# Windowed attention and an MLP-mixer: another order of operations and loads, and the last tail rows in two stores

## The chip, the cores and the metric

The kernel runs on one core of one Trainium2 chip. The metric is the device time of one execution in microseconds; the median of three runs stands for the kernel.

## The reference

Sliding-window attention with a linear bias, then a mixer block, for 8 batches of 576 rows, 8 heads of 64 (512 columns):

```python
scores = scale * np.matmul(q, k.transpose(0, 1, 3, 2))     # per batch and head, 576 x 576
mask = (rel >= 0) & (rel < 128)                             # rel = row - column
attn = softmax(np.where(mask, scores + bias[None], -1e9))
x = matmul(attn, v)                                         # back to (batch, 576, 512)
h = np.maximum(xt @ w_tok1, 0.0) @ w_tok2                   # token mix, 576 -> 256 -> 576
u = x + h.transpose(0, 2, 1)
h2 = np.maximum(u @ w_ch1, 0.0) @ w_ch2                     # channel mix, 512 -> 1536 -> 512
out = u + h2
```

## The kernel before

Work runs in blocks of 128 rows. A batch has 576 rows, four blocks and 64 rows over; the spare rows of two batches are joined into one tail block (`TAIL`), so two batches make a pair with nine blocks. All matmuls are in bf16.

For each batch there is a **side** part and a **main** part. The side part takes q and k of each block, transposes them (on TensorE in the opening, L653; later by SP's transposing transfers, L642), computes the scores of a block against itself and the block before it (L693, a 64-row form of the matmul, two heads at once), the exponentials on ScalarE (L716), the mask and bias as one product on DVE (L726), attention times v with a column of ones that gives the row sums (L760), and the normalisation (L773, L776; some of them on ScalarE, L782). Then comes the token mix: L805 and L815 (first layer), a ReLU (L823), L848 (second layer; L844 for the tail block) and the residual sum into the tile `ub` (L866). The tile is then transposed into `uT`, for batches 0 and 1 on TensorE (L883), from batch 2 on by SP (L874).

The main part is the channel mix. The first layer is L1045 (L1030 for the first pieces of batch 0, L967 for the last batch, L1088 for the tail), with its ReLU on L1051. The second layer uses seven half-size products in place of eight (L1234), with sums of the operands made on DVE (L1070) and the results collected in L1202; L1263 is the last product of the last batch, in two halves. The tail block's second layer is L1133, and L1140 adds its residual. Results leave by transfers at L1214, L1150 (tail rows) and L1270 (the last two blocks, one on SP's queue and one on ScalarE's).

Who comes first is not written by hand. A small planner (class `Plan`) holds every operation with its engine, a cost, a rank and its dependences, and plays them through in time: each engine takes the operation that can start first, ties going by rank. The rank is moved by a random offset per group of 30 operations, from the table `SEEDS`. The planner has costs for transfers: `LATE` and `RATES` for the loads that GpSimd (POOL) issues, `TURN` for SP's transposes (duration and lateness, for the uT and the qkT kind), `CASTS` for the first loads. The order that comes out is emitted as it is, one queue for each engine, and each engine then keeps to it. Where the planner expects TensorE to be idle in the first 60 us, it emits filler matmuls on zeros (`spin`, L1319).

POOL issues the loads in the order of the string `LOADS` (L378): `k1` is block 1 of k, `W1` and `W2` the token weights, `A0` to `A3` quarters of the first channel weight `WC1`, `B0` to `B3` of the second, `WC2`; then those of pairs 1 to 3 in a fixed order. At most eight of POOL's transfers are in flight. Each waits for its buffer: there are five for q and k and five for v.

SP's queue holds the transposes and most output stores, in the planner's order: an instruction whose data is not there holds up all behind it. The stores of the tail block go out as two transfers, because its 128 rows belong to two batches. In the last batch the tail block is the last in its list, so it comes in two column halves, with two stores for each.

Of the kernel before, what the change touches and what calls it, by code (L numbers as in the profile page):

```python
# [64 lines left out]
def offset(o):  # L65
    seed = SEEDS.get(o.group, 0)
    z, full = (seed << 20) + o.part * 1000 + o.at, (1 << 64) - 1
    z = (z + 0x9E3779B97F4A7C15) & full
    z = ((z ^ (z >> 30)) * 0xBF58476D1CE4E5B9) & full
    z = ((z ^ (z >> 27)) * 0x94D049BB133111EB) & full  # L70
    return ((z ^ (z >> 31)) >> 11) * 2.0**-52 - 1.0 if seed else 0.0


class Plan:
# [54 lines left out]
    def run(self):  # L129
# [43 lines left out]
        def advance(to):  # L173
            nonlocal clock, flying
            while True:
# [13 lines left out]
                if both:  # L189
                    rate = RATES[0 if not lines[1][0][1].bus else 2 if lines[1][0][1].bus < 1500 else 1]  # L190
                    if getattr(lines[0][0][1], "packets", 0) == 520:
# [18 lines left out]
        def send(o, at, line, work, late):  # L210
            nonlocal flying
            coming.append([at, line, work, o, late])
            flying += 1

        while todo:
# [70 lines left out]
            elif e == "SP":  # L286
                o.t0 = t
                if o.bus:
# [3 lines left out]
                    turns.append(o)  # L292
                    send(o, t + 300, 1, TURN[o.bus > 1500][0], TURN[o.bus > 1500][1])
                else:
                    free[e] = t + 590
                    send(o, t + 300, 1, STORE * o.cost / 550, 1010.0)
            else:
                o.t0 = t
                free[e] = t + o.cost
                send(o, t + o.cost, 0, STORE if o.packets < 0 else o.packets * PACKET, 1010.0 if o.packets < 0 else LATE[t > FETCH])  # L300
                lanes.append(o)
# [8 lines left out]
    def emit(self, spin):  # L310
# [11 lines left out]
        for _, _, go in sorted(work, key=lambda w: w[:2]):  # L322
# [20 lines left out]
RANKH = 0  # L343
RELU = 350
SUMS_AT = 60e3
SEEDS = {0: 846071, 4: 412855, 5: 343328, 6: 901394, 7: 671959, 8: 764867, 10: 416701, 11: 351752, 12: 70309, 20: 619675, 21: 120696, 22: 577973, 23: 405716, 30: 213057, 31: 165847, 32: 71954, 40: 404590, 41: 482568, 50: 286568, 51: 611926, 60: 579527, 61: 819459, 62: 379002, 70: 640395, 71: 934419, 72: 439456, 80: 109511, 81: 910233, 82: 748762, 90: 519950, 91: 197367, 101: 150347, 102: 405724, 110: 7956, 111: 36992, 112: 363882, 120: 129293, 122: 874736, 130: 359970, 131: 803027, 140: 23914, 141: 388902, 142: 496852, 150: 220523, 151: 220010, 152: 75231, 153: 900190}
GROUP = 30
SHIFT = 1500.0
UNIT_LATE = False
# [14 lines left out]
MORE = 150.0  # L364
START = 5200.0
RAW = 3
CASTS = [5000.0, 5680.0, 7560.0, 8040.0]
PACKET = 0.813
LATE = (2400.0, 3500.0)
FETCH = 9000.0  # L370
STORE = 774.0
TURN = [(792.0, 1267.0), (1380.0, 2400.0)]
RATES = [(0.37, 0.23), (0.52, 0.35), (0.47, 0.18)]
HALF = 0.9
EARLY = 1


LOADS = ("k1 q1 k2 q2 v0 k8 q8 v1 v2 v8 v3 W1 q7 q4 k4 W2 q6 "  # L378
         "k6 A0 k7 q5 A3 k5 v7 v4 A1 v6 v5 A2 B0 T0 P1 B2 B1 B3")


@with_exitstack
def kernel(
# [16 lines left out]
    P = nc.NUM_PARTITIONS  # L400
    B, H, S, D = q.shape
# [4 lines left out]
    NC = S // P  # L406
    R = S - NC * P
    NB = 2 * NC + 1
    TAIL = 2 * NC
# [24 lines left out]
    def bank(choice=ONE):  # L434
        return plan.buf("ps", choice)
# [27 lines left out]
    W1 = const.tile([P, NC, DTOK], BF16, name="W1")  # L463
    W1p = const.tile([P, 2, DTOK], BF16, name="W1p")
    W2 = const.tile([P, NJ, NC * P], BF16, name="W2")
# [75 lines left out]
    for i_, raw in enumerate(raws):  # L541
        buf, i = block(0, (0, RAW)[i_ // 2])["qk"], i_ % 2

        def cast(eng=dve_.tensor_copy, raw=raw, buf=buf, i=i):
            eng(out=buf()[:, i, :, :], in_=raw.rearrange("p (h d) -> p h d", h=H))

        plan.op("DVE", (520, 660)[i], cast, -100 + i_, makes=buf, after=CASTS[i_],
                **({"other": ("ACT", 600, lambda cast=cast: cast(act_.copy))} if i_ > 1 else {}))
# [4 lines left out]
    plan.items = []  # L553
    for item in LOADS.split():
        what, n = item[:-1], int(item[-1])
# [461 lines left out]
    def main(b, rank):  # L1017
        pr, half = b // 2, b % 2
# [5 lines left out]
        if b == 0:  # L1024
            first = [bank() for _ in range(PIECES)]
            for blk in blocks:
                for t, ct in enumerate(first):
                    def go(t=t, ct=ct, blk=blk):
                        for cb in range(NCB):
                            pe_.matmul(ct()[:, blk * P : (blk + 1) * P], lhsT=WC1[:, cb, t * P : (t + 1) * P],  # L1030
                                       rhs=uT()[:, cb, blk * P : (blk + 1) * P],
                                       start=cb == 0, stop=cb == NCB - 1)
# [89 lines left out]
        for blk in blocks:  # L1122
            cuts = [slice(0, DM)]
            if b == B - 1 and blk == blocks[-1]:
                cuts = [slice(0, DM // 2), slice(DM // 2, DM)]
            for cols in cuts:
                o2 = bank()
                n = cols.stop - cols.start
                for g in range(NHT // 3):
                    def go(blk=blk, g=g, o2=o2, cols=cols):  # L1130
                        for t in range(3 * g, 3 * g + 3):
                            l = r2t()[:, t, :] if blk == TAIL else r2()[:, t, (blk % NC) * P : (blk % NC + 1) * P]
                            pe_.matmul(o2()[:, cols], lhsT=l, rhs=WC2[:, t, cols], start=t == 0, stop=t == NHT - 1)  # L1133

                    rk = rank(648)
                    rd = [(r2t, g * 3 // 4), (r2t, (g * 3 + 2) // 4)] if blk == TAIL else [(r2, t) for t in range(3 * g, 3 * g + 3)]
                    plan.op("PE", 649 * n / DM, go, rk, reads=rd, needs=lc2[3 * g : 3 * g + 3],
                            **({"makes": o2} if g == 0 else {"adds": o2}))
                ob = plan.buf("ob")
                plan.op("DVE", 160 + 530 * n / DM, lambda blk=blk, o2=o2, ob=ob, cols=cols: dve_.tensor_tensor(  # L1140
                    out=ob()[:, cols], in0=o2()[:, cols], in1=ub()[:, blk, cols], op=ALU.add), rk, makes=ob, uses=[o2],
                    reads=[(ub, blk)])

                late = b >= FROM_P and blk not in blocks[-2:] or FROM_P <= b < B - 1
                q_ = nc.gpsimd if late else nc.sync

                def store(blk=blk, ob=ob, cols=cols, q_=q_):
                    if blk == TAIL:
                        for i in range(2):
                            q_.dma_start(out=out[2 * pr + i, NC * P : S, cols], in_=ob()[i * R : (i + 1) * R, cols])  # L1150
                    else:
                        q_.dma_start(out=out[b, (blk % NC) * P : (blk % NC + 1) * P, cols], in_=ob()[:, cols])

                if late:
                    plan.dma(store, P, -1, uses=ob)
                else:
                    plan.op("SP", 550, store, rk, uses=[ob])
# [197 lines left out]
```

## Time and profile before

| | |
|---|---|
| median of three runs | 278.48 us (277.51 to 278.57) |
| the profiled execution | 277.36 us |
| its span, first to last instruction | 275.6 us |
| instructions | 6968 |
| granted TensorE clock | 1.000 |
| read from and written to HBM | 35.85 MB, 9.44 MB |

The span is what the profile sees; the execution's time has 1.8 us around it. In the profile, PE is TensorE's matmuls, PEld its weight loads, POOL is GpSimd, and SPq is SP's queue. A row of a group gives the source line, engine, operation, tiles written and read, shape and count. A row of a timeline gives the start, the length, and in brackets the idle time of the engine before it. In a row of a line's operations, three times with slashes are the least, the middle and the greatest duration in ns. "DMA to landing" is the time from issue to the last byte's notice. A row of windows gives a stretch, its length, then busy time and count of PE, PEld, DVE, ACT and POOL, the granted clock, the DMA share and GB/s.

### The profile page before, as it was taken

Reading aid. Unit: us, or ns where it says so; the run is one execution under the profiler, and the core shown is the slowest. Engines: PE = TensorE matmul, PEld = TensorE weight load, DVE = VectorE, ACT = ScalarE, POOL = GpSimd, SP = SyncE. Lnnn points to the kernel's source line nnn. Section 1 sums busy time; section 2 is a strip of 40 time slices with the busy share of each in tenths; the row PEclk is TensorE's granted clock in tenths of the full one; section 3 lists DMA queues with packets and bytes.
Section 4 is the critical chain, followed back from the end, with each engine's and each line's share of the span. In section 5 each row is a group of like instructions: output and inputs, shape, how many; then the busy total and the mean of one; then the engine's idle time right before and its main releaser. Section 6 shows DMA issues by size and latency. Waiting matters only on the chain.

```text
span 275.6 us, 6968 instructions
## 1 busy us (share of the span) xinstructions
PE 268.4 (97%) x2790; PEld 180.8 (66%) x2824; DVE 210.3 (76%) x496; ACT 139.1 (50%) x239; POOL 114.0 (41%) x144
## 2 busy tenths in 40 slices
PE   8999999999999999999999999999999999999994
PEld 4665655676676556585658655576676655599983
DVE  7596799987898379956979468763998459967983
ACT  5475893426940388109950187116960089106560
POOL 8898747940454039700891009600462410021000
PEclk9999999999999999999999999999999999999999
DMA  8999999999899899979999859999599760043014
GB/s 156 154 165 178 179 200 183 155 129 210 127 107 130 176 233 142 152 120 193 189 149 148 199 146 95 135 158 242 68 99 126 195 132 0 2 113 137 1 49 145
DMA packets 167553, 38.71 MB, mean 140 GB/s; under 512 B 155808, under 2 KB 166688, under 8 KB 167520
## 3 DMA queue, kind: packets, MB, share of 16 engines
q0 software_dynamic: 114032, 19.77, 91.8%
q1 hardware_dynamic: 51264, 17.83, 33.4%
q10 hardware_dynamic: 2224, 0.66, 1.2%
q8 instruction: 22, 0.36, 0.5%
q14 instruction: 11, 0.09, 0.1%
HBM read 35.85 MB, written 9.44 MB: 164 GB/s over the span
## 4 chain that ended last, share of the span: by engine, by line
PE 81%; DMA 6%; DVE 5%; POOL 4%; issue 2%; SPq 1%; POOLq 0%
PE ps L1234 25%; PE ps L1045 24%; PE ps L760 6%; PE ps L693 5%; DMA qk<-in_k_dram 5%; PE ps L805 4%; PE ps L848 4%; PE ps L1088 4%; PE ps L967 3%; PE ps L1133 3%; DVE pe L726 2%; POOL qk L530 2%; POOL v L530 1%; DMA uT<-ub 1%; PE ps L815 1%
## 5 line engine op out<-in xcount | busy, mean ns | idle before, releaser
L1045 PE MATMUL ps<-uT,WC 128*128 128x512 bf16 x306 | 77.9, 379 | 1.3 <-DMA uT<-ub 0.2
L716 ACT ACTIVATE pe<-ps 128x1024 bf16<-128x1024 f32 (+1 forms) x76 | 63.4, 890 | 19.1 <-PE ps L693 18.8
L530 POOL DMA_DIRECT2D v<-in_v_dram x40 | 34.1, 858 | 91.8 <-PE ps L760 88.6
L1051 ACT ACTIVATE r<-ps 128x512 bf16<-128x512 f32 x77 | 45.0, 604 | 51.4 <-PE ps L1045 49.3
L1045 PEld LDWEIGHTS <-WC 128*128 128x128 bf16 x328 | 29.1, 98 | 29.3 <-issue 0.9
L726 DVE TENSOR_TENSOR pe<-pe,mask 128x1024 bf16<-128x1024 bf16 (+1 forms) x64 | 38.7, 609 | 12.0 <-ACT pe L716 11.5
L1234 PEld LDWEIGHTS <-r 128*128 128x128 bf16 x372 | 36.1, 98 | 7.3
L530 POOL DMA_DIRECT2D qk<-in_k_dram x38 | 33.0, 876 | 4.6 <-DMA WC<-in_moe_w_ch_dram 2.4
L530 POOL DMA_DIRECT2D qk<-in_q_dram x38 | 32.7, 866 | 1.7 <-PE ps L1234 0.7
L1234 PEld LDWEIGHTS <-s 128*128 128x128 bf16 x288 | 27.4, 98 | 6.0 <-issue 2.0
L776 DVE TENSOR_TENSOR xb<-ps,rt 128x256 bf16<-128x256 f32 (+1 forms) x72 | 28.9, 417 | 0.8
L760 PEld LDWEIGHTS <-pe 128*128 128x128 bf16 (+1 forms) x560 | 22.6, 98 | 9.1 <-DVE pe L726 1.3
L760 PE MATMUL ps<-v,pe 128*128 128x65 bf16 (+1 forms) x560 | 26.9, 194 | 0.3
L1234 PE MATMUL ps<-WC,r 128*128 128x256 bf16 x192 | 25.4, 273 | 0.0
L1234 PE MATMUL ps<-WT,s 128*128 128x256 bf16 x192 | 24.8, 273 | 0.0
L866 DVE TENSOR_TENSOR ub<-ps,xb 128x512 bf16<-128x512 f32 x34 | 21.3, 683 | 2.5 <-PE ps L848 2.5
L1234 PE MATMUL ps<-WT,r 128*128 128x256 bf16 x180 | 22.3, 273 | 0.0
L693 PEld LDWEIGHTS <-qkT 64*128 64x128 bf16 x560 | 14.8, 94 | 10.7 <-issue 8.2
L1202 DVE TENSOR_TENSOR raw<-ps,ub 128x512 f32<-128x512 f32 x22 | 15.0, 686 | 8.1 <-PE ps L1234 8.1
L693 PE MATMUL ps<-qkT 64*128 64x128 bf16 (+1 forms) x304 | 19.5, 216 | 0.0
L1093 ACT ACTIVATE r2t<-ps 128x512 bf16<-128x512 f32 x12 | 7.2, 600 | 22.9 <-PE ps L1088 22.7
L773 DVE RECIPROCAL rt<-ps 128x4 f32<-128x4 f32 (+1 forms) x76 | 12.6, 176 | 7.3 <-PE ps L760 6.9
(101 smaller groups left out, 348.1 us busy)
## 6 DMA issues: line engine op xcount, KB each, us to landing
out_dram<-raw SPq DMA_DIRECT2D x18, 256.0 KB, 2.8
v<-in_v_dram POOLq DMA_DIRECT2D x32, 128.0 KB, 5.1
qk<-in_k_dram POOLq DMA_DIRECT2D x30, 128.0 KB, 5.5
qk<-in_q_dram POOLq DMA_DIRECT2D x30, 128.0 KB, 5.1
WC<-in_moe_w_ch_dram POOLq DMA_DIRECT2D x8, 384.0 KB, 9.4
out_dram<-ob SPq DMA_DIRECT2D x5, 256.0 KB, 2.6
out_dram<-ob POOLq DMA_DIRECT2D x4, 256.0 KB, 2.7
out_dram<-raw POOLq DMA_DIRECT2D x4, 256.0 KB, 2.9
```

Source lines behind the costliest of these rows:

```text
L530: nc.gpsimd.dma_start(out=to()[p0 : p0 + n, :, :], in_=rows(src, b, s0, n))
L693: pe_.matmul(wide(e)[:, i, kind, a:z], lhsT=ts[kb]()[e * D : (e + 1) * D, NHP + i, :], rhs=ts[blk]()[e * D : (e + 1) * D, i, a:z], start=n ...
L716: act_.activation(out=pb()[:, e, :, lo:, c0:c1_], in_=wide(e)[:, :, lo:, c0:c1_], func=ACT.Exp, scale=scale)
L726: dve_.tensor_tensor(out=o, in0=o, in1=heads(mk, es), op=ALU.mult)
L760: pe_.matmul(view()[a:z, at, i, :], lhsT=pb()[:, e, i, kind, a:z], rhs=vb()[:, h, 0 : D + 1], start=m == 0, stop=m == len(mms) - 1, skip_g ...
L773: dve_.reciprocal(out=rt()[r0:r1_, 0:n, :, :], in_=view()[r0:r1_, :, :, D : D + 1])
L776: dve_.tensor_tensor(out=x4(), in0=view()[r0:r1_, :, :, 0:D], in1=rt()[r0:r1_, 0:n, :, :].broadcast_to([r1_ - r0, n, 4, D]), op=ALU.mult)
L866: plan.op("DVE", 690, lambda blk=blk, ht=ht, hs=hs: dve_.tensor_tensor(out=ub()[:, blk, :], in0=ht()[:, hs], in1=xb()[:, blk, :], op=ALU.a ...
L1045: pe_.matmul(ct()[:, :], lhsT=WC1[:, cb, t * P : (t + 1) * P], rhs=uT()[:, cb, :], start=cb == 0, stop=cb == NCB - 1)
L1051: plan.op("ACT", 600, lambda t=t, ct=ct: act_.activation(out=r2()[:, t, :], in_=ct()[:, :], func=ACT.Relu), rk, part=(r2, t), uses=[ct], o ...
L1202: dve_.tensor_tensor(out=v, in0=both(bk), in1=src, op=ALU.add)
L1234: pe_.matmul(of(bk, c), lhsT=l(t, c), rhs=w(t), start=first, stop=g == 1 and t == HK - 1, skip_group_check=True)
```

## The change

Three kinds of edit: the table of seeds, which moves ranks and so the order of the operations; some of the planner's costs and the order of the first loads; and the tail store of the last batch, which becomes one transfer for both batches of the pair.

```diff
-SEEDS = {0: 846071, 4: 412855, 5: 343328, 6: 901394, ...}
+SEEDS = {0: 210116, 4: 311062, 5: 744428, 6: 487106, ...}
...
-CASTS = [5000.0, 5680.0, 7560.0, 8040.0]
+CASTS = [4950.0, 5600.0, 7500.0, 8000.0]
 PACKET = 0.813
-LATE = (2400.0, 3500.0)
+LATE = (2400.0, 3300.0)
...
-TURN = [(792.0, 1267.0), (1380.0, 2400.0)]
-RATES = [(0.37, 0.23), (0.52, 0.35), (0.47, 0.18)]
+TURN = [(843.0, 2200.0), (1455.0, 2000.0)]
+RATES = [(0.2, 0.45), (0.47, 0.31), (0.5, 0.13)]
...
-LOADS = ("k1 q1 k2 q2 v0 k8 q8 v1 v2 v8 v3 W1 q7 q4 k4 W2 q6 "
-         "k6 A0 k7 q5 A3 k5 v7 v4 A1 v6 v5 A2 B0 T0 P1 B2 B1 B3")
+LOADS = ("k1 q1 q2 k2 k8 v8 v0 q8 v1 v3 v2 W1 q4 k4 W2 k7 q6 "
+         "q7 A0 k5 k6 v4 A2 v7 q5 A3 v6 P1 T0 v5 A1 B0 B3 B1 B2")
...
                 def store(blk=blk, ob=ob, cols=cols, q_=q_):
-                    if blk == TAIL:
+                    if blk == TAIL and b == B - 1:
+                        q_.dma_start(out=out[2 * pr : 2 * pr + 2, NC * P : S, cols], in_=ob()[:, cols])
+                    elif blk == TAIL:
                         for i in range(2):
                             q_.dma_start(out=out[2 * pr + i, NC * P : S, cols], in_=ob()[i * R : (i + 1) * R, cols])
```

The whole table of seeds is new; what that does can only be seen in the order that comes out. The two added lines move every line behind them by two: L1214 becomes L1216, L1234 becomes L1236, L1319 becomes L1321, and the tail store of the last batch is L1149.

More of the change, by code (lines that the diff above doesn't have):

```diff
@@ L345 @@
 SUMS_AT = 60e3
-SEEDS = {0: 846071, 4: 412855, 5: 343328, 6: 901394, 7: 671959, 8: 764867, 10: 416701, 11: 351752, 12: 70309, 20: 619675, 21: 120696, 22: 577973, 23: 405716, 30: 213057, 31: 165847, 32: 71954, 40: 404590, 41: 482568, 50: 286568, 51: 611926, 60: 579527, 61: 819459, 62: 379002, 70: 640395, 71: 934419, 72: 439456, 80: 109511, 81: 910233, 82: 748762, 90: 519950, 91: 197367, 101: 150347, 102: 405724, 110: 7956, 111: 36992, 112: 363882, 120: 129293, 122: 874736, 130: 359970, 131: 803027, 140: 23914, 141: 388902, 142: 496852, 150: 220523, 151: 220010, 152: 75231, 153: 900190}
+SEEDS = {0: 210116, 4: 311062, 5: 744428, 6: 487106, 7: 50177, 10: 146866, 11: 515882, 12: 973009, 20: 155072, 21: 744920, 22: 317240, 23: 698122, 30: 985153, 31: 625367, 32: 450301, 40: 930871, 41: 214279, 42: 112853, 50: 891528, 51: 242028, 60: 755591, 61: 792979, 62: 375085, 70: 685210, 71: 980520, 72: 835065, 80: 583261, 81: 958126, 90: 935583, 91: 899083, 100: 196181, 101: 365479, 102: 47195, 110: 147652, 111: 54013, 112: 364482, 120: 45674, 121: 471640, 122: 625263, 130: 763037, 131: 347222, 140: 294247, 141: 509518, 142: 314107, 150: 245247, 151: 898266, 152: 34723, 153: 834918}
 GROUP = 30
```

## The prediction

> **What bounds the kernel now.** I read the page first (span, busy shares, slices, chain), then the waits of TensorE, then the windows and timelines of the places that the change touches.
>
> ```profile
> span 275.6 us, 6968 instructions
> ...
> PE 268.4 (97%) x2790; PEld 180.8 (66%) x2824; DVE 210.3 (76%) x496; ACT 139.1 (50%) x239; POOL 114.0 (41%) x144
> ...
> PE   8999999999999999999999999999999999999994
> ...
> PEclk9999999999999999999999999999999999999999
> ...
> PE 81%; DMA 6%; DVE 5%; POOL 4%; issue 2%; SPq 1%; POOLq 0%
> ```
>
> TensorE is busy in 97% of the span, at the full granted clock, in every slice but the first and the last. A busy PE is not proof of work without gaps, since a matmul's modelled tail covers short ones, so I asked for all waits of PE:
>
> ```profile
> PE ps L1319 <- DVE zero L494: 1.0, 1, 1.0
> PE ps L1045 <- DMA uT<-ub: 0.2, 1, 0.2
> ```
>
> One microsecond before the first filler, and 0.2 us on a transposed tile. Nothing else. The stretch after the last matmul is the other idle piece:
>
> ```profile
> 270.00:275.00 5.00, 1.62 (x15) 1.21 (x13) 1.33 (x4) 0.00 (x0) 0.00 (x0) 1.00 0.52 164
> ```
>
> So the kernel is a solid block of PE work from about 1.0 to 271.6 us, and 4 us of tail. An order of operations can remove waits, fillers and tail; it cannot remove the block. That is why I expect little in either direction from the order alone.
>
> **The change, part by part.** The program lists show what moves. All the real matmuls are there in equal number and size. TensorE switches into and out of its 64-row form equally often (46 times each way). DVE has 495 instructions for 496 and ScalarE 245 for 241: one normalisation went from DVE to four short operations on ScalarE.
>
> ```profile
> L782 ACT ACTIVATE xb<-ps,rt x16: 300/326/362, 18.1 to 109.8; 128x64 bf16<-128x64 f32 x12, 64x64 bf16<-64x64 f32 x4
> ```
>
> ScalarE is 50% busy, so I cost them at nothing; uncovered, four would be at most 1.3 us of delay. POOL keeps 144. SP has two transfers fewer.
>
> 1. *Fillers* (matmuls on zeros, L1319). There are 44 for 42, with 18,656 columns for 17,868.
>
> ```profile
> L1319 PE MATMUL ps<-zero x42: 266/364/594, 1.0 to 22.8; 128*128 128x460 bf16 x8, 128*128 128x444 bf16 x5, 128*128 128x400 bf16 x5, 128*128 128x492 bf16 x4
> 94.29 1.90 PE L1045 MATMUL ps<-uT,WC 128*128 128x512 bf16 x8
> ```
>
> Eight matmuls of 512 columns take 1.90 us; less the modelled 0.38 us of the last one that is 0.217 us each, 0.42 ns a column. 788 columns more cost 0.33 us if TensorE is never held up by anything else there; if the columns only fill time in which it would wait for a load, they cost nothing. I take **+0.3 us** of 0 to 0.35.
>
> 2. *Order of the loads.* The opening is paced by loads as well as by PE:
>
> ```profile
> PEld L1030 <- DMA WC<-in_moe_w_ch_dram: 0.2, 1, 0.2
> PEld L848 <- DMA W<-in_moe_w_tok_dram: 0.2, 1, 0.2
> 27.05 0.62 PE L1030 MATMUL ps<-uT,WC 128*128 128x128 bf16 x8
> 19.89 0.81 POOL L534 DMA_DIRECT2D WC<-in_moe_w_ch_dram  x1
> ```
>
> Two stages on PE start when a weight transfer ends their wait, each after 0.2 us: the loads arrive just in time. The first quarter of WC1 (A0) is the 19th item of both lists, with one W1, one W2 and 16 q, k or v blocks ahead of it, so it should land at the same time, and from the first matmul that uses it (L1030) to the end both programs hold the same columns. No gain can come from there. W2 goes one block earlier, v0 three transfers later, and its first use also goes later. I cost it at nothing. If that cover is gone, one 128 KB block out of place is about 0.8 us, POOL's own issue time in the last row.
>
> 3. *Lead of the transposed tiles.* This is what the new costs for SP and the new seeds move. After a batch's last L848 matmul, DVE adds the residual, SP transposes four or five tiles (L874), and only then can the first-layer matmuls (L1045, in the last batch L967) start. I counted the PE columns between these two points at the pace above, for batches 2 to 7: before 5.9, 7.8, 11.3, 7.6, 7.8, 8.3 us, after 6.5, 8.5, 7.4, 8.9, 10.6, 8.9 us.
>
> ```profile
> 85.83 6.00 SPq L874 DMA_TRANSPOSE uT<-ub  x4
> 86.38 0.59 PE L848 MATMUL ps<-r,W 128*128 128x512 bf16 x2
> 93.01 1.02 PE L1045 MATMUL ps<-uT,WC 128*128 128x512 bf16 x4 [0.17 <-DMA uT<-ub]
> 174.67 1.46 PE L848 MATMUL ps<-r,W 128*128 128x512 bf16 x6
> 183.83 1.46 PE L1045 MATMUL ps<-uT,WC 128*128 128x512 bf16 x5
> ```
>
> Batch 2 had 6.0 us from 86.97 to 93.01 and waited 0.17; batch 5 had 7.7 us and did not visibly wait. Five of six leads grow by 0.6 to 2.8 us. The shown wait should go: **-0.2 us**. Next in line there is the row of second-layer matmuls, which PE has in plenty. Batch 4 alone loses 3.9 us of lead:
>
> ```profile
> 144.76 1.24 PE L848 MATMUL ps<-r,W 128*128 128x512 bf16 x5
> 145.84 2.50 SPq L874 DMA_TRANSPOSE uT<-ub  x2
> 150.36 0.37 SPq L1214 DMA_DIRECT2D out_dram<-raw  x1
> 150.78 1.58 SPq L874 DMA_TRANSPOSE uT<-ub  x1
> 152.66 0.37 SPq L1214 DMA_DIRECT2D out_dram<-raw  x1
> 153.08 1.21 SPq L874 DMA_TRANSPOSE uT<-ub  x1
> DMA to landing us min/median/max: 2.3/4.3/6.5
> ```
>
> Before, two output stores stood between its transposes on SP's queue and held it from 148.3 to 150.4 us. After, all four transposes stand together. Issued 1.25 us apart, as the first two, the last goes out at 149.6 us and lands 2.3 to 4.3 us later, 151.9 to 153.9, which is 5.9 to 7.9 us after 146.0 against a lead of 7.4. So 0 to 0.5 us of new wait here, behind which every L1045 of the batch queues.
>
> 4. *Other new waits.* From a full score block to its first use in L760, the least lead is 1.9 us before and 1.7 us after; in the row below such waits were short.
>
> ```profile
> PEld L760 <- DVE pe L726: 1.3, 5, 0.3
> ```
>
> Together with batch 4 and the opening I take **+0.4 us** for new waits, of 0 to 1.3 (the upper end: batch 4's 0.5 and one load block of 0.8).
>
> 5. *Tail rows of the last batch.* Each column half is now one store on SP instead of two.
>
> ```profile
> 270.84 1.11 SPq L1150 DMA_DIRECT2D out_dram<-ob  x2
> 271.00 0.42 DVE L1267 TENSOR_TENSOR raw<-ps,ub 128x256 f32<-128x256 f32 x1 [0.23 <-PE ps L1263]
> 272.04 0.56 SPq L1270 DMA_DIRECT2D out_dram<-raw  x1
> 272.12 0.36 ACTq L1270 DMA_DIRECT2D out_dram<-raw  x1
> out_dram<-ob SPq DMA_DIRECT2D x2, 64.0 KB, 2.4
> out_dram<-raw SPq DMA_DIRECT2D x1, 128.0 KB, 2.2
> out_dram<-raw ACTq DMA_DIRECT2D x1, 128.0 KB, 1.8
> L1350 SPq EVENT_SEMAPHORE  x9: 17/28/28, 274.3 to 275.0; - x9
> L1350 SPq DRAIN  x2: 7/7/7, 274.8 to 274.8; - x2
> ```
>
> SP's last store has its data at 271.42 but is issued at 272.04, behind two tail stores of 0.56 us each, and lands at 272.04 + 2.2 = 274.25. One issue fewer lets it go at about 271.5 and land at 273.7; the store on ScalarE's queue, at 272.12 + 1.8 = 273.9, is then last: 0.35 us sooner. SP then waits in turn for the eight semaphores that these transfers use, from 274.3 to the drain at 274.8, 0.06 us each. The program lists give the two last stores the first two of the eight before, and the last two after. The other six waits then pass while the last store is on its way: another 0.35 us. **-0.7 us**, provided that one store of 128 rows in two pieces lands like its neighbours (2.2 to 2.4 us). The trace of before has no store of that shape; the near rows are these, so I take them. The first rival is the other end.
>
> **Sum**: +0.3 - 0.2 + 0.4 - 0.7 = -0.2 us. The profiled execution took 277.36 us (1.8 more than its span), so its like would be 277.2. The median of the three runs shown is 278.48, 1.1 above it, and the profile cannot say what those runs spent it on. If it is late transfers, the longer leads cover it; if not, the change keeps it. I take half: **277.7 us**, 0.3% under the median. A measurement of this kernel tells about 0.5% from no change.
>
> **Rivals.**
>
> *A, the merged store is slow (slower).* Its side in DRAM begins with a dimension of two batches, where every other store begins with 64 or 128 rows. If the rows are dealt to DMA engines by that first dimension, two engines carry 64 rows of 1 KB each, instead of 16 engines 8 each.
>
> ```profile
> q1 hardware_dynamic: 272, 0.26, 15.7%
> 267.24 1.12 SPq L1150 DMA_DIRECT2D out_dram<-ob  x2
> 268.77 1.69 SPq L1214 DMA_DIRECT2D out_dram<-raw  x2
> ```
>
> The first row is SP's queue from 263 to 268 us: 272 packets in 15.7% of 16 engines times 5 us, 46 ns each. The second merged store then needs 64 x 46 ns = 2.9 us beyond some 1.9 us fixed, and the last store's 8 packets follow on the same two engines: 270.84 + 1.9 + 3.3 = 276.1 us. If the first one (issued near 267.2) and the two 256 KB stores between them pile up too, it is 267.24 + 1.8 + 168 x 46 ns = 276.8. That is 1.8 to 2.5 us after 274.25; less the 0.35 of semaphore waits, the tail costs 1.5 to 2.2 instead of -0.7, and with the same half of the gap the time is 279.9 to 280.6, say **280.1**. It decides as soon as the second merged store lands after ScalarE's at 273.9: from about 24 packets an engine, five engines or fewer. For it: the pattern as the program writes it. Against it: no transfer in the trace shows it. The Trainium skill, page "DMA: Bandwidth & Descriptors", section "Why a DMA increments its semaphore by 16 and not by 1", states this rule: the number of engines is the largest up to 16 that divides the slowest dimension above one of both sides, here two. By that rule the time is this rival's; the traces shown can neither bear it out nor refute it.
>
> *B, the new order waits (slower).* Batch 4's 0.5 us, one load block of 0.8 us late in the opening, and a second one behind it: 2 us where I took 0.4, **279.3**. For it: the just-in-time loads. Against it: the equal bytes ahead of A0, and five longer leads.
>
> *C, the late transfers were the gap (faster).* No new waits, and the whole 1.1 us goes: 277.2 - 0.4 = **276.8**. For it: batch 2 waited and batch 5 is close. Against it: only 0.2 us of such waiting is in the profile.
>
> That the change doesn't do what it says would be C's opposite, leads that grow where nothing was late, and lies inside the forecast.
>
> **How the numbers follow.** Forecast 0.46, A 0.30, B 0.12, C 0.12. The forecast's own range, with the unknown waits (0 to 1.3) and the gap gone or kept, is 276.8 to 279.2; A reaches 280.6 and C 276.8 or a little less, so 276.6 to 280.4 leaves out about 2 in 10. Under 277.09 (0.5% faster): C and 0.05 of the forecast, 0.17. Over 279.87: two thirds of A (if the whole gap goes, A is 279.4 to 280.1) and 0.07 of B, 0.27. The rest, 0.56, is within.
>
> **What would show it.** Fillers: the first L1030 matmul 0.2 to 0.3 us later than 27.05. Leads: no wait of L1045 on uT, and batch 4's first L1045 not late. Tail: the second L1149 issue taking 0.56 us, SP's last store issued by 271.6 and landing before ScalarE's. Rival A: landing times of L1149 near 5 us instead of 2.4, and a longer stretch from the last matmul to the end than 4.0 us. I am wrong if PE shows more than a microsecond of waits in the opening or in batch 4.

## The result, and the profile after

| | median | lowest to highest | runs |
|---|---|---|---|
| before | 277.78 us | 276.95 to 278.57 | 6 |
| after | 280.79 us | 280.45 to 282.4 | 6 |

The ratio is 1.012, with a 95% interval of 1.0085 to 1.0155: the change made the kernel slower by 3.0 us. The forecast of 277.7 was wrong, and 280.79 lies above its range too.

The page of after, read as the page of before was:

```profile
span 278.5 us, 6958 instructions
...
PE 267.9 (96%) x2792; PEld 180.8 (65%) x2826; DVE 212.2 (76%) x495; ACT 140.6 (50%) x243; POOL 113.9 (41%) x144
...
PE   8999999999999999999999999999999999999990
...
PEclk9999999999999999999999999999999999999998
...
PE 81%; DMA 5%; DVE 4%; ACT 3%; POOL 3%; issue 2%; POOLq 0%; ACTq 0%
```

The span has grown by 3.0 us (2.96 before rounding), the profiled execution by 3.1 (280.45 for 277.36). PE's work and its clock are as before; what is new is the 0 in the last slice, where before had a 4. The shares of the chain that ended last are nearly those of before and do not show the loss: 3 us are 1% of the span. It is behind the last matmul. The window of after in which the last matmul ends (the prediction shows the same window of before):

```profile
270.00:275.00 5.00, 1.60 (x14) 1.09 (x12) 1.35 (x4) 0.00 (x0) 0.00 (x0) 1.00 0.57 179
```

TensorE is busy for 1.60 of these 5 us, before for 1.62: in both programs it ends 1.6 us into the window, at 271.60 and 271.62. The two programs are level there. The tail, by which I mean the stretch from the end of the last matmul to the end of the span, is 6.95 us instead of 3.97. The timeline of SP in the last 12 us (start, length, instruction):

```profile
266.48 0.37 SPq L1216 DMA_DIRECT2D out_dram<-ob  x1
267.41 0.64 SPq L1149 DMA_DIRECT2D out_dram<-raw  x1
268.33 0.37 SPq L1216 DMA_DIRECT2D out_dram<-ob  x1
270.11 0.37 SPq L1216 DMA_DIRECT2D out_dram<-raw  x1
270.68 0.54 SPq L1149 DMA_DIRECT2D out_dram<-raw  x1
271.47 0.69 SPq L1272 DMA_DIRECT2D out_dram<-raw  x1
```

SP does what was forecast: one issue less, and the last store leaves at 271.47 instead of 272.04. The list of transfers of after from 269 to 279 us (tiles, queue, KB, median us from issue to landing) shows what then happens:

```profile
out_dram<-raw SPq DMA_DIRECT2D x1, 256.0 KB, 3.5
out_dram<-raw SPq DMA_DIRECT2D x2, 128.0 KB, 6.1
out_dram<-ob ACTq DMA_DIRECT2D x1, 128.0 KB, 3.6
```

The two of 128 KB on SP's queue are the second merged store and the last store behind it. The views give no landing time for the merged stores, so the 6.1 is the last store's; it took 2.2 us before. Its source line gives the greater of the two last stores' times, and the waits of SP at the end of the program, L1352, end with it:

```profile
DMA to landing us min/median/max: 3.6/4.9/6.1
```
```profile
L1352 SPq EVENT_SEMAPHORE  x11: 17/28/28, 272.2 to 278.5; - x11
L1352 SPq DRAIN  x3: 7/7/13, 277.7 to 278.0; - x3
```

271.47 + 6.1 = 277.6, and the drain follows at 277.7. How the transfers ran is in the transfers' own bandwidth, in 40 slices, of the last 4 us before that landing:

```profile
GB/s 41 41 41 31 41 31 10 0 31 51 51 41 61 41 51 51 41 51 51 41 51 51 41 51 51 41 51 51 41 61 41 41 61 41 21 31 20 0 0 0
...
DMA packets 160, 0.15 MB, mean 39 GB/s; under 512 B 9, under 2 KB 160, under 8 KB 160
...
q1 hardware_dynamic: 135, 0.13, 10.7%
```

But for a short gap, mostly 40 to 50 GB/s go on to the end of the transfers at 277.2. SP's queue moves 135 packets in 10.7% of 16 engines times 4 us, 51 ns each. One engine with a 1 KB packet every 51 ns is 20 GB/s, so the row is the rate of two engines.

The trace also keeps the moments at which the completion semaphore of a store is raised, and these count the parts into which a store is dealt. Each of the last eight stores of before raised it 16 times, none earlier than 1.5 us behind its issue. In after each merged store raised it once, about 1.0 us behind its issue, and then only twice: at 272.17 and 272.29, and at 276.92 and 277.23. That is 4.9 and 6.6 us behind the two issues. The last store on SP's queue raised it 14 times by 273.56, and the last two times at 277.25 and 277.56. Fourteen of its sixteen parts were in time, and two waited behind the merged store.

### The profile page after: what moved, and what is told of

It reads as the page before. It is cut to its first block, busy times and chain, and to the rows that moved or that the text cites. A ratio compares the mean times of both kernels' runs of the same rounds, so it can differ in the third digit from the quotient of the medians.

```text
span 278.5 us, 6958 instructions
## 1 busy us (share of the span) xinstructions
PE 267.9 (96%) x2792; PEld 180.8 (65%) x2826; DVE 212.2 (76%) x495; ACT 140.6 (50%) x243; POOL 113.9 (41%) x144
## 4 chain that ended last, share of the span: by engine, by line
PE 81%; DMA 5%; DVE 4%; ACT 3%; POOL 3%; issue 2%; POOLq 0%; ACTq 0%
PE ps L1236 26%; PE ps L1045 22%; PE ps L760 6%; PE ps L693 5%; PE ps L848 4%; PE ps L1088 4%; PE ps L805 4%; PE ps L1133 4%; PE ps L967 3%; DMA qk<-in_k_dram 3%; DMA qk<-in_q_dram 2%; POOL qk L530 2%; ACT pe L716 2%; ACT r L1051 1%; DVE pe L726 1%
## 5 line engine op out<-in xcount | busy, mean ns | idle before, releaser
L1045 PE MATMUL ps<-uT,WC 128*128 128x512 bf16 x305 | 76.7, 379 | 0.9
L1045 PEld LDWEIGHTS <-WC 128*128 128x128 bf16 x328 | 29.1, 97 | 29.0
L1236 PEld LDWEIGHTS <-r 128*128 128x128 bf16 x372 | 35.7, 98 | 6.7 <-issue 0.7
L1236 PEld LDWEIGHTS <-s 128*128 128x128 bf16 x288 | 27.7, 98 | 6.6 <-issue 1.3
L760 PEld LDWEIGHTS <-pe 128*128 128x128 bf16 (+1 forms) x560 | 23.4, 98 | 9.2 <-DVE pe L726 0.9
L1236 PE MATMUL ps<-WC,r 128*128 128x256 bf16 x192 | 25.4, 273 | 0.1
L1236 PE MATMUL ps<-WT,s 128*128 128x256 bf16 x192 | 24.5, 273 | 0.0
L1236 PE MATMUL ps<-WT,r 128*128 128x256 bf16 x180 | 22.4, 273 | 0.0
L1204 DVE TENSOR_TENSOR raw<-ps,ub 128x512 f32<-128x512 f32 x19 | 13.0, 688 | 7.4 <-PE ps L1236 7.0
```

Of the source, the lines that this page charges most:

```text
L760: pe_.matmul(view()[a:z, at, i, :], lhsT=pb()[:, e, i, kind, a:z], rhs=vb()[:, h, 0 : D + 1], start=m == 0, stop=m == len(mms) - 1, skip_g ...
L1045: pe_.matmul(ct()[:, :], lhsT=WC1[:, cb, t * P : (t + 1) * P], rhs=uT()[:, cb, :], start=cb == 0, stop=cb == NCB - 1)
L1204: dve_.tensor_tensor(out=v, in0=both(bk), in1=src, op=ALU.add)
L1236: pe_.matmul(of(bk, c), lhsT=l(t, c), rhs=w(t), start=first, stop=g == 1 and t == HK - 1, skip_group_check=True)
```

## The experiments

Each time stands beside runs of the kernel before on the same chip. The diffs are against the kernel before where they say so, else against after.

**One half of the change at a time.** `e1_order_alone` is after with the four tail stores of before (a line with ... stands for lines left out, here and below):

```diff
-                    if blk == TAIL and b == B - 1:
-                        q_.dma_start(out=out[2 * pr : 2 * pr + 2, NC * P : S, cols], in_=ob()[:, cols])
-                    elif blk == TAIL:
+                    if blk == TAIL:
```

> The new order, seeds and loads with the old four tail stores. Theory T (the merged store lands late because its rows go to two DMA engines; the order is neutral): like the kernel before, 277.8 us within 0.5, span end about 4.0 us after the last matmul. Rival O (the new order costs the 3 us): 280.8 us. Rival M (one store of 128 rows is slow whatever its shape): as T here.

`e2_store_alone` is before with only the merged stores:

```diff
-                    if blk == TAIL:
+                    if blk == TAIL and b == B - 1:
+                        q_.dma_start(out=out[2 * pr : 2 * pr + 2, NC * P : S, cols], in_=ob()[:, cols])
+                    elif blk == TAIL:
```

> The old order with the merged tail stores alone. T and M: 2.5 to 3.2 us slower than the kernel before, 280.3 to 281.0 us, with last landing near 277.5 us after the start and the PE block ending at 271.6 as before. O: within 0.5 us of the kernel before, or 0.7 faster.

Measured: the order alone 277.95, ratio 1.0016 (1.0005 to 1.0026), tail 3.94 us; the stores alone 280.05, a little under the 280.3 expected at least, ratio 1.0085 (1.0068 to 1.0101), tail 6.37 us. So the stores cost 2.4 us in the old order as well, and the new order costs 0.2%, 0.3 to 0.4 us. Together that is 2.7 to 2.8 us, inside the interval of the change (2.4 to 4.3). The last transfers of the second kernel:

```profile
out_dram<-raw SPq DMA_DIRECT2D x1, 128.0 KB, 5.5
out_dram<-raw ACTq DMA_DIRECT2D x1, 128.0 KB, 5.0
```

Even the store on ScalarE's queue, which was not touched and took 1.8 us before, takes 5.0. It shares no queue with the merged stores. Its semaphore was raised 14 times by 275.38 and the last two times at 276.61 and 277.19, so here too two parts of sixteen come last. That fits DMA engines that both queues share. The other fourteen parts were 1.2 to 1.4 us later than in before as well; why is not shown.

**The shape of the merged store.** `e3_rows_first` issues the same two transfers of the same bytes, with the 64 rows as the first dimension in DRAM and the two batches behind it. It puts the tail rows of the last pair into wrong places, so it serves for timing only:

```diff
-                        q_.dma_start(out=out[2 * pr : 2 * pr + 2, NC * P : S, cols], in_=ob()[:, cols])
+                        q_.dma_start(out=out[2 * pr : 2 * pr + 2, NC * P : S, cols].rearrange("i r c -> r i c"), in_=ob()[:, cols])
```

> The changed kernel with the two dimensions of the merged store exchanged on the DRAM side: 64 rows first, then the 2 batches. It writes the tail rows of the last pair to the wrong places; the bytes, rows and count of transfers are those of the changed kernel. T: the store lands 2.0 to 2.6 us after its issue, the tail is 0.7 us shorter than in the kernel before (0.35 from SP's last store going out sooner, 0.35 from the last semaphores), 277.1 us. M: as slow as the changed kernel, 280.8. O: 280.0 or more.

Measured: 277.04, ratio 0.9973 (0.9958 to 0.9988), tail 3.13 us. Landing times of L1149, then of L1272 in this kernel:

```profile
DMA to landing us min/median/max: 2.1/2.2/2.2
```
```profile
DMA to landing us min/median/max: 1.7/1.7/1.8
```

Each merged store now raises its semaphore 16 times, from 1.9 to 2.2 us behind its issue. Between this kernel and after only the order of two dimensions differs; 3.75 us of the median go, and 3.8 us of the tail. This carries the verdict: neither the single transfer nor its size is slow, but the dimension of two in front.

**A length in place of a shape.** If the number of engines comes from what divides the first dimension, then 62 rows, whose largest divisor up to 16 is 2, must be slow too, in a plain store of one batch; 60 rows (15) must not. Both kernels are before with shorter last tail stores (60 in the second), which leave the last rows of each tail unwritten:

```diff
+                            z = NC * P + (62 if b == B - 1 else R)
-                            q_.dma_start(out=out[2 * pr + i, NC * P : S, cols], in_=ob()[i * R : (i + 1) * R, cols])
+                            q_.dma_start(out=out[2 * pr + i, NC * P : z, cols], in_=ob()[i * R : i * R + z - NC * P, cols])
```

> The kernel before, with the four tail stores of the last batch cut from 64 to 62 rows each; it leaves out the last two rows of each tail. Theory T as the page's rule puts it (engines = the largest number up to 16 that divides the leading dimension; 62 gives 2): each store puts 31 packets on two engines, a pair as many as one merged store, so about as slow as the merged store alone: 279.5 to 280.1 us. Rival D (the loss comes from the dimension of two batches itself, or its large stride): 277.7 us within 0.4.

> The same with 60 rows, four left out of each tail. T: 15 divides 60, so 15 engines carry 4 packets each: 277.7 us within 0.4, landing 2.0 to 2.6 us after issue. D: the same.

Measured: 62 rows 280.75, ratio 1.0112 (1.009 to 1.0135); 60 rows 277.59, ratio 0.9994 (0.9977 to 1.0012). L1271, the last stores behind them, with 62 rows:

```profile
DMA to landing us min/median/max: 4.8/4.9/5.0
```

and with 60:

```profile
DMA to landing us min/median/max: 2.0/2.1/2.1
```

Two rows of 64 left out, and the kernel is 3 us slower; four left out, and it is as before. Bytes and queues of the two kernels are nearly the same, so this leaves the division of the rows among engines, and the semaphores count it. Each of the last four tail stores raises its semaphore once about 0.5 us behind its issue; with 60 rows 15 raises follow, from 1.3 us on, and with 62 rows only two, at 3.0 to 5.1 us. Against 16 with 64 rows and two for the merged store, these are the largest divisors up to 16 of 60, 62, 64 and 2.

The 280.75 lies above the 279.5 to 280.1 that were expected. The tail of the profiled execution, 6.59 us, is only 0.2 longer than in e2; the rest is not explained.

**Which of the two merged stores it is.** Both are before with only one of the two column halves merged: `and cols.start` in the condition for the second half, `and not cols.start` for the first.

> The kernel before, with only the second column half of the last tail merged and the first as two stores. T with packets of the first store and of the two stores behind it piling up on the two engines: about half of the loss, 278.7 to 279.1 us. T without piling up (only the last store counts): 280.0 us, as with both merged.

> The kernel before, with only the first column half of the last tail merged. T: its 64 packets keep two engines busy from about 268.5 to 271.5 us; the two 256 KB stores behind it queue 16 packets each there, so they end near 273, and the last stores are held up little: 277.7 to 278.3 us. If each merged store cost the same: 278.9 us.

Measured: the last half merged 279.67, ratio 1.0066 (1.0043 to 1.0088); the first half 277.39, ratio 0.9991 (0.9973 to 1.0009). The one lies between the two times that were expected for it, the other below those expected. The transfers at the end, last half merged:

```profile
out_dram<-raw SPq DMA_DIRECT2D x1, 128.0 KB, 4.3
out_dram<-raw ACTq DMA_DIRECT2D x1, 128.0 KB, 4.1
```

first half merged:

```profile
out_dram<-raw SPq DMA_DIRECT2D x2, 256.0 KB, 3.8
out_dram<-raw SPq DMA_DIRECT2D x1, 128.0 KB, 2.4
out_dram<-raw ACTq DMA_DIRECT2D x1, 128.0 KB, 2.1
```

A merged store issued over 4 us ahead of the end of the last matmul is slow (its last raise comes 5.0 us behind the issue) and slows the 256 KB stores beside it (3.8 us, before 2.4), but it is out of the way in time and costs nothing. The last one costs 1.8 us, and both 2.4: by these the first adds 0.5 or so, which would be the packets that it leaves on the two engines, though the two intervals overlap.

**The issue gain by other means.** The forecast had 0.7 us here: half because the last store waits in SP's queue behind two tail stores, half from the order of the semaphores. Four kernels take work off that queue or reorder it while every transfer keeps its 64 or 128 rows. `e4_two_queues` (on the order of e1) and `e7_two_fewer` (on before) give the second tail store to ScalarE's queue; e7 also moves the tail stores of batch 1 to POOL's, so that the order of the semaphores at the end changes.

```diff
-                            q_.dma_start(out=out[2 * pr + i, NC * P : S, cols], in_=ob()[i * R : (i + 1) * R, cols])
+                            q2 = nc.gpsimd if b == 1 else nc.scalar if b == B - 1 and i else q_
+                            q2.dma_start(out=out[2 * pr + i, NC * P : S, cols], in_=ob()[i * R : (i + 1) * R, cols])
```

(e4 has only `nc.scalar if b == B - 1 and i else q_`.)

> The new order, with each pair of tail stores of the last batch on two queues, the first on SP's and the second on ScalarE's. T: SP's last store goes out 0.5 us sooner and lands by 273.8, so the end follows ScalarE's store at 273.9: 0.3 us less than the order alone, 277.5 us. O: 280.5. M: as T.

> The kernel before, in its order, with the second store of each last tail half on ScalarE's queue, and the tail stores of batch 1 (at about 98 us) moved from SP's queue to POOL's, so that the two last stores of the kernel take the last two of the eight semaphores instead of the first two. T: 0.3 us from SP's last store going out sooner and 0.35 from the semaphores, 277.0 to 277.1 us, with POOL idle enough at 98 us to hide its two stores. If the semaphores cost nothing: 277.4.

Measured: 277.72, ratio 0.9999 (0.9987 to 1.0011), and 277.48, ratio 0.9993 (0.9976 to 1.001). No gain over before can be told, where 277.5 and 277.0 to 277.1 had been expected. The tails of the two profiled executions are shorter all the same: 3.48 us in e4 (3.94 in e1) and 3.61 in e7 (3.97 in before). In e4 SP's last store left at 272.19, 0.1 us ahead of the end of the last matmul. In e7 that part of the gain did not come:

```profile
271.36 0.49 ACTq L1151 DMA_DIRECT2D out_dram<-ob  x1
271.39 1.05 SPq L1151 DMA_DIRECT2D out_dram<-ob  x1
272.54 0.54 SPq L1271 DMA_DIRECT2D out_dram<-raw  x1
```

SP's issue took 1.05 us, for about 0.56 in before, and its last store left 0.4 us after the last matmul, no sooner than before. That two queues issue at the same moment does not explain it, for in e4 they did so too:

```profile
271.40 0.47 SPq L1151 DMA_DIRECT2D out_dram<-raw  x1
271.40 0.50 ACTq L1151 DMA_DIRECT2D out_dram<-raw  x1
```

Why the one issue was long stays open. What did come in e7 is the gain on the semaphores: SP's drain follows the last landing by 0.1 us, in before by 0.5.

`e8_swapped` (on before) and `e9_swapped_new` (on the order of e1) keep the tail stores on SP and let the two last stores change queues, so that the one whose data is there first leaves through ScalarE's free queue. Batch 1's tail stores go through POOL here too.

```diff
...
-                (nc.sync, nc.scalar)[c].dma_start(out=out[b, HS + c * P : HS + (c + 1) * P, 0:HN], in_=ob()[:, 0:HN])
+                (nc.scalar, nc.sync)[c].dma_start(out=out[b, HS + c * P : HS + (c + 1) * P, 0:HN], in_=ob()[:, 0:HN])
```

> The kernel before, with the two queues of the last two blocks exchanged (the first goes out on ScalarE's queue, the very last on SP's, after its tail stores) and batch 1's tail stores moved to POOL, so that the last two stores take the last two semaphores. Expected from the tails so far: the stretch from the last matmul to the end 3.2 to 3.4 us in place of 4.0, 277.0 to 277.1 us. If stores issued together on both queues slow each other, as they did with the second tail store on ScalarE's queue, 3.6 us and 277.4.

> The same two edits on the new order with the old four tail stores. Theory: the order alone plus the shorter tail, 277.2 to 277.4 us, so no better than the same edits on the old order.

Measured: 277.26, ratio 0.9986 (0.9971 to 1.0001), tail 3.73, and 277.06, ratio 0.9981 (0.9965 to 0.9998), tail 3.35. e8 stayed behind the 277.0 to 277.1 that it was built for; e9 came out below its expected 277.2 to 277.4. The end of e9:

```profile
270.83 1.12 SPq L1151 DMA_DIRECT2D out_dram<-raw  x2
271.60 0.36 ACTq L1271 DMA_DIRECT2D out_dram<-raw  x1
272.24 0.35 SPq L1271 DMA_DIRECT2D out_dram<-ob  x1
```

SP's two tail issues and ScalarE's store now lie beside each other, and SP's last store follows at 272.24. By its median this is the fastest version that computes the whole reference, 0.02 to 0.35% under before by its interval; that of e8 overlaps it. e3 is level with it, at 277.04.

**The fillers.** `e10_less_filler` is e1 with fewer filler columns, 17,056 for 18,656, 0.67 us of PE work:

```diff
-                        fills.append((a, i, (z - a + MORE) * 1.2 if a < CHILLY else (z - a - (60 if a > DENSE else 0)) * 2.4))
+                        fills.append((a, i, (z - a + MORE) * 1.2 if a < CHILLY else (z - a - (60 if a > DENSE else 0)) * 2.1))
```

> The new order with the old four tail stores and the fillers after the first cold ones cut by an eighth, 17,056 columns for 18,656, all else alike. If the opening is bound by TensorE's own work (the fillers' term of the prediction), 0.4 to 0.7 us less than the order alone: 277.3 to 277.5. If it is bound by the loads, the first L1030 matmul does not move: 277.9 to 278.0.

Measured: 277.78, ratio 1.0002 (0.9985 to 1.0018); e1, beside its own runs of before, had 1.0016 (1.0005 to 1.0026). The result lies between the two that were expected, and the intervals overlap: by them e10 is about 0.4 us faster than e1, give or take 0.5. The run does not settle how much of the opening is PE's work.

## Why the prediction was wrong, point by point

1. *Fillers, +0.3, and new waits, +0.4.* With the 0.2 gained on the leads the order was forecast at +0.5; alone it measured 0.3 to 0.4. The sum held; its parts are not separated by any run, so that may be luck. (The step has v0 three transfers later. In POOL's order it is four, the 9th issue for the 5th; it was costed at nothing.) Of the waits, two of 0.3 us came, both in the opening. The waits of PE in after:

```profile
PE ps L1321 <- DVE zero L494: 1.0, 1, 1.0
PE ps L653 <- DMA qk<-in_k_dram: 0.3, 1, 0.3
PE ps L653 <- DVE qk L545: 0.3, 1, 0.3
```

The first L1030 of after begins at 27.4, for 27.05:

```profile
L1030 PE MATMUL ps<-uT,WC x32: 219/219/230, 27.4 to 30.9; 128*128 128x128 bf16 x32
```

That is the sign named for the fillers, but these two waits explain it as well, and e10 does not tell them apart. One execution cannot give this sign at all, as point 5 shows.

2. *Leads of the transposed tiles, -0.2.* Right in its direction. In none of the six profiled executions of the new order (after, e1, e3, e4, e9, e10) does L1045 wait for `uT`. But in the eight of the old order (before, e2, e5 to e8) the wait stands in only two, 0.2 us in before and 0.4 in e6_first_half, so that the 0.2 was the wait of one execution and not its usual size. Batch 4, which lost lead, in after:

```profile
149.06 5.68 SPq L874 DMA_TRANSPOSE uT<-ub  x4
...
157.29 0.60 PE L1045 MATMUL ps<-uT,WC 128*128 128x512 bf16 x2
```

The four transposes stand together and the first layer starts 2.5 us after the last of them was issued, with no idle time in brackets: the 0 to 0.5 us put on this batch were 0.

3. *Tail, -0.7.* This is the step that failed: "provided that one store of 128 rows in two pieces lands like its neighbours (2.2 to 2.4 us)". The first merged store and the last piled up on two engines, and the tail grew by 3.0 us. I took the value of the near rows, though none of them had a first dimension under 64, and the store's pattern stood in the diff. The other parts of the step, the issue and the semaphores, were right: with the same two transfers in a better shape (e3) the tail is 3.13 us, 0.84 less than in before. ScalarE's store is last there, at 272.08 + 1.7 = 273.8, for 274.25 in before, and the drain follows it at once, where before took 0.5 us more:

```profile
L1352 SPq DRAIN  x3: 7/7/12, 273.9 to 274.2; - x3
```

4. *Rival A* had the mechanism and the place, and gave 280.1. Its tail was too small: last landing at 276.1 to 276.8, measured 277.6. It counted 168 packets of 46 ns on each of the two engines. There are 176, since ScalarE's store gives them 8 more, and at the mean of 51 ns of the window above they take 9.0 us instead of 7.7. Behind the first issue at 267.41 that leaves 1.2 us for the start and the notice. The sign that it named, landings of L1149 near 5 us, came: 4.9 and 6.6 by the semaphores. The rule from the Trainium skill that stood beside it (page "DMA: Bandwidth & Descriptors", section "Why a DMA increments its semaphore by 16 and not by 1") could not be borne out by the trace of before. The runs now agree with it: a first dimension of 2 or 62 in the store just ahead makes the last stores land after 3.6 to 6.1 us, one of 64 or 60 after 1.7 to 2.3, and the late raises of the semaphores are 2, 2, 16 and 15.

5. *The 1.1 us between the profiled execution and the median*, of which I took half. The median of six runs of before is 277.78, so the gap was 0.4 and mostly a matter of three runs. What varies is the opening, far more than the transposes: e6_last_half has before's order, and the waits of PE in its first 30 us are

```profile
PE ps L848 <- DMA W<-in_moe_w_tok_dram: 0.5, 1, 0.5
PE ps L653 <- DVE qk L545: 0.2, 1, 0.2
PE ps L653 <- DMA qk<-in_q_dram: 0.2, 1, 0.2
```

with the first L1030 at 27.9:

```profile
L1030 PE MATMUL ps<-uT,WC x32: 219/219/230, 27.9 to 31.6; 128*128 128x128 bf16 x32
```

The 0.9 us of waits are about what it starts late, and it ends its matmuls at 272.46, 0.8 us later than the profile of before. The eight profiled executions of the old order show the same: the four with the earliest first L1030 (26.9 to 27.2) end their matmuls at 271.6 to 271.7, the four others (27.4 to 27.9) at 272.0 to 272.5. That speaks against rival C, whose longer leads cover late transposes; what is late here is the loads. How often each opening occurs stays open.

6. *Rival B* (2 us of waits) did not come: the order alone is at +0.2%.

## What to carry to other kernels

Before two transfers are joined into one, look at the first dimension of the joined access pattern: a small one, or a length with no large divisor up to 16, as 2 and 62 here, concentrates the store on few DMA engines, and whatever is queued on those engines behind it is late too. A saved issue of half a microsecond is only worth something if the transfer still spreads. Where a transfer's shape occurs nowhere in the trace, do not price it by the nearest rows and leave the other end to a rival; the pattern in the code is evidence.

## What the runs showed of the hardware

- Into how many parts a store is dealt shows in the late raises of its semaphore: 16 with 64 rows in front, 15 with 60, and two with 62 rows or with two batches in front. For the two, the rate is that of two engines.
- One DMA engine kept up a 1 KB packet every 51 ns on the mean; on two engines that is 40 to 50 GB/s, where the stores at the end of e3 run at over 350 in the fullest slices. The transfers of e3 from 269 to 275 us:

```profile
GB/s 164 137 362 396 382 375 96 0 0 0 0 0 0 212 341 369 341 362 123 212 341 280 157 341 328 89 143 389 314 28 0 0 0 0 0 0 0 0 0 0
```

- A slow transfer delays transfers of other queues: ScalarE's last store took 5.0 us in e2 for 1.8 in before, though nothing else was on its queue at that time.
